# Expert MLPs with 608 slots each, six row buffers, and the router's logits and transpositions in one step

## The chip, the cores and the metric

The kernel runs on 1 core of one Trainium2 chip. The metric is device time in microseconds of one execution; before the change three runs were taken, and their median counts. Engines are named as in the profile: PE (TensorE matmuls), PEld (its weight loads), DVE (VectorE), ACT (ScalarE), POOL (GpSimd), SP (SyncE, which issues DMAs).

## The reference

Three layers follow each other, in fp32. Inputs: q, k, v of shape 4 x 8 x 576 x 64, a gated MLP with w_a, w_b (512 x 1536) and w_out (1536 x 512), and eight experts with w1 (512 x 1024) and w2 (1024 x 512) each.

```python
scores = scale * np.matmul(q, k.transpose(0, 1, 3, 2))
scores = np.where(masks[None, :, :, :], scores, -1000000000.0)   # heads 0-3 local, 4-7 strided
attn = np.exp(scores - np.max(scores, axis=-1, keepdims=True))
attn = attn / (np.sum(attn, axis=-1, keepdims=True) + 1e-09)
x = np.matmul(attn, v)                                            # as 2304 rows of 512
x = (x @ w_a) * (x @ w_b) @ w_out
noisy_logits = x @ w_gate + np.log1p(np.exp(x @ w_noise)) * noise
top2 = np.argpartition(-noisy_logits, 2, axis=1)[:, :2]
...
out[mask] += top2_w[mask, k, None] * (np.maximum(x[mask] @ w1[e], 0.0) @ w2[e])
```

Each of the 2304 tokens goes to its two best experts of eight, with softmax weights over the two; 576 tokens per expert on average.

## The kernel before, in words

**Products.** Every large product is made of three fp32r matmuls (`mm3`, L194 to L198): each operand is split into a high and a low part, and hi x hi (L196), lo x hi (L197) and hi x lo (L198) are summed. ACT makes the high part, DVE the low one.

**First stage.** Tokens are cut into five chunks: c = 0 to 3 hold the first 512 tokens of a batch, c = 4 holds the 64 last tokens of the four batches (256 columns). For each chunk, f runs over 12 blocks of the hidden width: `stage_a` (L691) makes pa and pb (12 matmuls each), whose product is split into gh and gl, and `stage_b` (L716) of the block before adds to the output po. `ORDER` (L557) gives the sequence. PE's order is written by hand in this stage; the order of ACT, DVE, POOL and SP is planned by a scheduler that works with its own model of durations. After pa, after pb and after po comes a call of `point()` (L797): it takes one step of attention (`attq`), one of `finq` (or a second of attention), and one of `bgq` (two in the last chunk). These queues hold generators; a step ends at a `yield`.

**Router.** When a chunk's rows are out, `finish(c, rows)` (L425) is put on `finq`. For each of the chunk's J tiles (four, two in the last chunk) it transposes the rows (four transposes into a PSUM tile of tag t, which has two buffers; copied to x2T by DVE or ACT, L432 to L437) in one step, and multiplies with the gate weights in the next (L441, copied to lg by DVE at L442). `route` (L446) then follows: a chain of small DVE and ACT operations that gives the two best experts of each token and their weights, up to ms (L478); after three yields the ranking product (L485) counts places within each expert; then slots are worked out (L489 to L507) and POOL scatters token numbers and weights into `table` in DRAM (L510). For the last chunk the experts 0 and 1 start at slot 384 or later (GAP), so that their tiles 0 to 2 can be fetched before it.

**Experts.** Each expert has CAP = 640 slots, five tiles of 128. `fetch` reads the table (L757, SP), gathers the rows of each tile from x2 (L763, POOL), transposes them (L772) and splits them into hi and lo (L773, L774). Tiles 0 to 2 are group 0 (384 columns), tiles 3 and 4 group 1 (256 columns). `passes` (L859) lists the work: the experts 0 and 1 go by groups in four passes (0: expert 0, tiles 0 to 2; 1: expert 1, the same; 2 and 3: the tiles 3 and 4 of both), the experts 2 to 6 in one pass each, and the last expert in two, the tiles 3 and 4 at the very end. In a pass, for each of 8 blocks f, `mm1` (L863) makes ph for each group (12 matmuls with the group's columns moving) and splits relu(ph) into hh (ACT, L872) and hl (DVE, L873); `mm2` (L878) follows LAG = 2 blocks later with three matmuls of 512 columns for each tile, the tile's 128 columns of hh and hl as weights. At the last block the row tile y is scaled (L894 DVE, L896 ACT; three buffers) and added to the output by a scatter on POOL (L897). In this stage the scheduler plans PE's order too.

**Weights.** `load_expert` (L731) reads w1 and w2 in pieces of 512 KB into two st buffers (L156, SP) and splits them (L159 ACT, L160 DVE); it runs on `bgq`, for expert 0 from c = 4, f = 4 on. Slots above CAP would be done by `overflow_tile` (L928), one tile at a time, if any expert has more tokens than CAP; a count decides at the end (L909, L920).

Of the kernel before, what the change touches and what calls it, by code (L numbers as in the profile page):

```python
# [20 lines left out]
NT = 2304  # L21
LAG = 2
PAD = 1024
CAP = 640
# [8 lines left out]
def attention_moe_kernel(ctx: ExitStack, tc: tile.TileContext, q, k, v, w_a, w_b, w_out,  # L33
# [15 lines left out]
    table = tc.dram_tile([E * NT, 2], I32, name="table")  # L49
# [16 lines left out]
    limit = cpool.tile([1, (NT - CAP) // 128], F32, name="limit")  # L66
# [13 lines left out]
    with tc.tile_pool(name="setup", bufs=1) as sp:  # L80
# [20 lines left out]
        nc.gpsimd.iota(base, pattern=[[NT, 8]], base=0, channel_multiplier=0,  # L101
                       allow_small_or_imprecise_dtypes=True)
        nc.gpsimd.iota(base0, pattern=[[NT, 8]], base=0, channel_multiplier=0,
                       allow_small_or_imprecise_dtypes=True)
        nc.gpsimd.iota(limit, pattern=[[128, (NT - CAP) // 128]], base=CAP, channel_multiplier=0,
# [16 lines left out]
    def late_setup():  # L122
        nrow = E * NT // 128
# [301 lines left out]
    def finish(c, rows):  # L425

        T0, J = tile_of(c)
        lg = rpool.tile([128, J, 16], F32, name="lg", tag="lg")
        for j in range(J):
            ps = pt([128, KD, 128])  # L430
            for kd in range(KD):
                nc.tensor.transpose(ps[:, kd, :], rows[j][:, 128 * kd:128 * kd + 128], ident)  # L432
            x2T = rpool.tile([128, KD, 128], F32, name="x2T", tag="x2T")
            if j % 2:
                nc.vector.tensor_copy(x2T, ps)
            else:
                nc.scalar.activation(x2T, ps, AF.Copy)  # L437
            yield
            ps = pt([128, 16])
            for kd in range(KD):  # L440
                nc.tensor.matmul(ps, x2T[:, kd, :], wg[:, kd, :], start=(kd == 0), stop=(kd == KD - 1))  # L441
            nc.vector.tensor_copy(lg[:, j, :], ps)  # L442
            yield
        yield from route(c, lg)

    def route(c, lg):  # L446
# [32 lines left out]
        yield  # L479
        yield  # L480
        yield
# [5 lines left out]
        if c == NCH - 1:  # L487
            for e in range(2):
                nc.vector.tensor_scalar(base[:, e:e + 1], base[:, e:e + 1], float(e * NT + GAP), None, op0=OP.max)  # L489
# [251 lines left out]

    def xset(e, g):
        n = 3 if g == 0 else 2
        p = xpool[e % 2, g]
        if (e, g) not in XS:
            t = f"x{g}{e % 2}"
            if p is rpool:
                both = p.tile([128, 2, KD, 128 * n], F32R, name=t, tag="row")
                XS[e, g] = (both[:, 0], both[:, 1])
                return XS[e, g]  # L750
            XS[e, g] = (p.tile([128, KD, 128 * n], F32R, name=t + "h", tag=t + "h"),
                        p.tile([128, KD, 128 * n], F32R, name=t + "l", tag=t + "l"))
        return XS[e, g]

    def load_table(e, t0, n):
        tb = rpool.tile([128, n, 2], I32, name="tb", tag="tb", bufs=6)
# [266 lines left out]
```

## Time and profile before

| what | value |
| --- | --- |
| runs | median 1139.32 us of 3 (1137.73 to 1145.32) |
| profiled execution, its own time | 1142.42 us |
| its span | 1140.6 us |
| granted TensorE clock, mean | 0.961 of full |
| instructions | 16116 |
| DMA | 105.02 MB, mean 92 GB/s |

The span runs from the first to the last instruction that the profile shows; the 1.8 us between it and the execution's own time lie around it. In the profile's rows times are microseconds from the span's start, and a mean duration is in ns. Matmuls are pipelined, so a matmul's drawn length overlaps the next one's; the pace is read from start to start. A row of the timeline may merge several like instructions (x8), and in square brackets it names how long the engine was idle before and what ended that.

### The profile page before, as it was taken

To read this page: it belongs to the slowest core of one execution; us is meant where nothing else is said; L and a number is where in the kernel's file an instruction comes from. 1 tells how busy PE (TensorE), PEld (TensorE's weight loads), DVE (VectorE), ACT (ScalarE), POOL (GpSimd) and SP (SyncE) were. 2 spreads that over 40 slices of the span, in tenths; PEclk is the share of its full clock that TensorE was granted. 3 is DMA by queue.
4 is the path that set the end of the run, shared out by engine and by line. 5 is a ranking of instruction groups with operands and counts; after the bars stand their busy time and mean duration, and the time that the engine had idled before them with its cause. 6 is when DMAs were issued, how large, how long until landed. Compare 5 with 4: busy or idle time off the path is not lost.

```text
span 1140.6 us, 16116 instructions
## 1 busy us (share of the span) xinstructions
PE 1097.2 (96%) x6411; PEld 929.8 (82%) x6411; DVE 511.5 (45%) x1075; ACT 432.3 (38%) x935; POOL 141.8 (12%) x136
## 2 busy tenths in 40 slices
PE   6989999999999999999997899989999999999996
PEld 4767777887778877888887799978999999999995
DVE  5849777735545444323135552245343334342211
ACT  4767877422333322212124532244242324241110
POOL 0000000002000020002002123221121313131111
PEclk7579999999999999999998999998999999999998
DMA  9535434200212021900003434266254635442123
GB/s 187 131 99 169 144 109 144 79 22 13 57 37 70 12 53 41 330 29 2 1 37 111 151 109 75 43 194 172 83 121 119 129 112 121 120 122 37 21 29 47
DMA packets 88549, 105.02 MB, mean 92 GB/s; under 512 B 43664, under 2 KB 48400, under 8 KB 88464
## 3 DMA queue, kind: packets, MB, share of 16 engines
q1 hardware_dynamic: 78352, 82.89, 24.5%
q0 software_dynamic: 10112, 21.02, 10.2%
q8 instruction: 52, 0.85, 0.3%
q14 instruction: 33, 0.27, 0.1%
HBM read 78.53 MB, written 25.35 MB: 91 GB/s over the span
## 4 chain that ended last, share of the span: by engine, by line
PE 81%; DVE 7%; DMA 6%; ACT 3%; issue 1%; another core or an unknown queue 1%; SPq 1%; POOL 0%; ACTq 0%; POOLq 0%; DVEq 0%
PE ph L196 6%; PE ph L198 6%; PE ph L197 6%; PE py L196 6%; PE py L197 6%; PE py L198 6%; PE pa L196 4%; PE pb L196 4%; PE po L196 4%; PE pb L197 4%; PE pb L198 4%; PE pa L197 4%; PE pa L198 4%; PE po L198 4%; PE po L197 4%; PE tt L290 2%
## 5 line engine op out<-in xcount | busy, mean ns | idle before, releaser
L873 DVE SCALAR_TENSOR_TENSOR hl<-ph,hh 128x256 fp32r<-128x256 f32 (+1 forms) x128 | 62.3, 489 | 213.9 <-ACT hh L872 212.6
L872 ACT ACTIVATE hh<-ph 128x256 fp32r<-128x256 f32 (+1 forms) x128 | 55.2, 433 | 225.0 <-PE ph L198 222.5
L708 DVE TENSOR_TENSOR a<-a,pb 128x512 f32<-128x512 f32 (+1 forms) x60 | 37.9, 632 | 130.5 <-PE pb L198 124.8
L897 POOL DMA_INDIRECT out_dram<-y,tb x40 | 64.0, 1600 | 185.7 <-ACT y L896 144.8
L510 POOL DMA_INDIRECT table<-pay,sli x36 | 35.1, 975 | 411.3 <-DVE sli L498 384.2
L703 ACT ACTIVATE a<-pa 128x512 f32<-128x512 f32 (+1 forms) x60 | 33.1, 551 | 120.4 <-PE pa L198 118.2
L763 POOL DMA_INDIRECT g<-x,tb x40 | 40.1, 1003 | 192.1 <-PE tt L772 170.0
L709 ACT ACTIVATE gh<-a 128x512 fp32r<-128x512 f32 (+1 forms) x60 | 35.1, 586 | 70.7 <-DVE a L708 57.2
L710 DVE TENSOR_TENSOR gl<-a,gh 128x512 fp32r<-128x512 f32 (+1 forms) x60 | 38.1, 635 | 20.0 <-ACT gh L709 18.8
L290 PEld LDWEIGHTS tt<-kT,qT 64*72 64x72 f32 (+1 forms) x336 | 29.5, 149 | 13.4 <-issue 10.3
L290 PE MATMUL tt<-kT,qT 64*72 64x72 f32 (+1 forms) x336 | 37.6, 253 | 1.1 <-ACT pT L336 1.1
L196 PE MATMUL py<-w6h,hh 128*128 128x512 f32 x80 | 32.3, 406 | 4.0 <-ACT hh L872 4.0
L336 ACT ACTIVATE pT<-tt 128x288 f32<-128x288 f32 (+1 forms) x64 | 24.9, 408 | 28.7 <-PE tt L335 28.7
L196 PE MATMUL pa<-xh,w0h 128*128 128x512 f32 (+1 forms) x80 | 32.7, 408 | 1.6 <-ACT xh L414 1.4
L335 PE MATMUL tt<-ident,s 72*72 72x72 f32 (+1 forms) x224 | 29.4, 263 | 4.2 <-DVE s L327 2.1
L335 PEld LDWEIGHTS tt<-ident,s 72*72 72x72 f32 (+1 forms) x224 | 22.3, 140 | 12.6 <-ACT qT L262 2.9
L196 PE MATMUL pb<-xh,w4h 128*128 128x512 f32 (+1 forms) x80 | 31.5, 394 | 0.6 <-issue 0.6
L197 PE MATMUL py<-w6l,hh 128*128 128x512 f32 x80 | 32.0, 400 | 0.0
L196 PE MATMUL pb<-xh,w1h 128*128 128x512 f32 (+1 forms) x80 | 31.9, 399 | 0.0
L196 PE MATMUL py<-w3h,hh 128*128 128x512 f32 x80 | 31.8, 398 | 0.0
L196 PE MATMUL py<-w2h,hh 128*128 128x512 f32 x80 | 31.8, 399 | 0.0
L196 PE MATMUL pa<-xh,w3h 128*128 128x512 f32 (+1 forms) x80 | 31.6, 395 | 0.0
(294 smaller groups left out, 3283.6 us busy)
## 6 DMA issues: line engine op xcount, KB each, us to landing
st<-in_moe_w_dram SPq DMA_DIRECT2D x64, 512.0 KB
out_dram<-zero SPq DMA_DIRECT2D x13, 512.0 KB
raw<-in_moe_w_a_dram SPq DMA_DIRECT2D x4, 1024.0 KB
raw<-in_moe_w_b_dram SPq DMA_DIRECT2D x4, 1024.0 KB
raw<-in_moe_w_out_dram SPq DMA_DIRECT2D x4, 1024.0 KB
x<-row SPq DMA_DIRECT2D x16, 256.0 KB
raw<-in_moe_w_a_dram SPq DMA_DIRECT2D x4, 512.0 KB
raw<-in_moe_w_b_dram SPq DMA_DIRECT2D x4, 512.0 KB
```

Of the source, the lines that this page charges most:

```text
L196: nc.tensor.matmul(ps, w[0], x[0], start=start, stop=False)
L197: nc.tensor.matmul(ps, w[0], x[1], start=False, stop=False)
L198: nc.tensor.matmul(ps, w[1], x[0], start=False, stop=stop)
L290: nc.tensor.matmul(ps[:, ii, :], self.qT[r0:r0 + 64, q0:q0 + n], self.kT[r0:r0 + 64, k0:k0 + m], start=not pemask, stop=not pemask or ii = ...
L335: nc.tensor.transpose(ps[:, ii, :], self.s[half][:, x, ii, :], ident[:n, :n])
L510: ins = nc.gpsimd.indirect_dma_start(out=table, out_offset=bass.IndirectOffsetOnAxis(ap=sli[:, 2 * j + kk:2 * j + kk + 1], axis=0), in_=pa ...
L708: nc.vector.tensor_mul(a, a, pb)
L710: behind[0] = nc.vector.tensor_sub(gl, a, gh.bitcast(F32))
L763: nc.gpsimd.indirect_dma_start(out=g, out_offset=None, in_=x2, in_offset=bass.IndirectOffsetOnAxis(ap=TB[e, t][:, 0:1], axis=0))
L872: nc.scalar.activation(hh, ph, AF.Relu)
L873: nc.vector.scalar_tensor_tensor(hl, ph, 0.0, hh.bitcast(F32), op0=OP.max, op1=OP.subtract)
L897: ins = nc.gpsimd.indirect_dma_start(out=out, out_offset=bass.IndirectOffsetOnAxis(ap=TB[e, t][:, 0:1], axis=0), in_=y, in_offset=None, co ...
```

## The change

1. CAP goes from 640 to 608, so tile 4 of each expert holds 96 rows and group 1 has 224 columns. `rows_of` and `WIDTH` give the sizes; table reads, gathers, transposes, splits, mm1, mm2, scaling and scatters use them. Each expert has 2400 places in the table instead of 2304, and the table's fill and the overflow's limits follow. `load_table` reads whole tiles with one DMA and tile 4 with its own.
2. The row tiles y have six buffers instead of three; the overflow's h takes a buffer of `ring` instead of its own.
3. In `finish`, the logits of one tile and the transposition of the next are one step, for every chunk: five steps for four tiles instead of eight, three for two instead of four. In `route`, the ranking product of c = 3 comes six yields after ms instead of three. Before steps of `first` (expert 0's fetch) are taken, `finq` is emptied.
4. At the very end, the two blocks of mm2 that are left are done tile by tile instead of block by block.

```diff
-CAP = 640
+CAP = 608
+SLOTS = 2400
...
-    table = tc.dram_tile([E * NT, 2], I32, name="table")
+    table = tc.dram_tile([E * SLOTS, 2], I32, name="table")
...
         lg = rpool.tile([128, J, 16], F32, name="lg", tag="lg")
-        for j in range(J):
-            ps = pt([128, KD, 128])
-            for kd in range(KD):
-                nc.tensor.transpose(ps[:, kd, :], rows[j][:, 128 * kd:128 * kd + 128], ident)
-            x2T = rpool.tile([128, KD, 128], F32, name="x2T", tag="x2T")
-            if j % 2:
-                nc.vector.tensor_copy(x2T, ps)
-            else:
-                nc.scalar.activation(x2T, ps, AF.Copy)
-            yield
-            ps = pt([128, 16])
-            for kd in range(KD):
-                nc.tensor.matmul(ps, x2T[:, kd, :], wg[:, kd, :], start=(kd == 0), stop=(kd == KD - 1))
-            nc.vector.tensor_copy(lg[:, j, :], ps)
+        x2T = None
+        for j in range(J + 1):
+            if j:
+                ps = pt([128, 16])
+                for kd in range(KD):
+                    nc.tensor.matmul(ps, x2T[:, kd, :], wg[:, kd, :], start=(kd == 0), stop=(kd == KD - 1))
+                nc.vector.tensor_copy(lg[:, j - 1, :], ps)
+            if j < J:
+                ps = pt([128, KD, 128])
+                for kd in range(KD):
+                    nc.tensor.transpose(ps[:, kd, :], rows[j][:, 128 * kd:128 * kd + 128], ident)
+                x2T = rpool.tile([128, KD, 128], F32, name="x2T", tag="x2T")
+                if j % 2:
+                    nc.vector.tensor_copy(x2T, ps)
+                else:
+                    nc.scalar.activation(x2T, ps, AF.Copy)
             yield
         yield from route(c, lg)
...
         ms = rpool.tile([128, J, 8], BF, name="ms", tag="ms")
         nc.vector.tensor_add(ms, oh[:, :, 0, :], oh[:, :, 1, :])
-        yield
-        yield
-        yield
+        for _ in range(6 if c == B - 1 else 3):
+            yield
         rk = pt([128, J + 1, 8])
...
+    def rows_of(t):
+
+        return min(128, CAP - 128 * t) if t >= 0 else 128
+
+    WIDTH = [384, CAP - 384]
+
     def xset(e, g):
-        n = 3 if g == 0 else 2
+        n = WIDTH[g]
...
-    def load_table(e, t0, n):
-        tb = rpool.tile([128, n, 2], I32, name="tb", tag="tb", bufs=6)
-        nc.sync.dma_start(tb, table[e * NT + 128 * t0:e * NT + 128 * (t0 + n), :].rearrange("(p t) c -> p t c", t=n))
-        for i in range(n):
-            TB[e, t0 + i] = tb[:, i, :]
+    def load_table(e, tiles):
+
+        whole = [t for t in tiles if rows_of(t) == 128]
+        for some in (whole, [t for t in tiles if rows_of(t) < 128]):
+            if some:
+                n, m, r0 = len(some), rows_of(some[0]), e * SLOTS + 128 * some[0]
+                tb = rpool.tile([128, n, 2], I32, name="tb", tag="tb" if some is whole else "tb4", bufs=5)
+                nc.sync.dma_start(tb[:m], table[r0:r0 + m * n, :].rearrange("(p t) c -> p t c", t=n))
+                for i, t in enumerate(some):
+                    TB[e, t] = tb[:m, i, :]
...
     def gather(e, t):
         g = xpool["g"].tile([128, DM], F32, name="g", tag="g", bufs=GB[0])
-        nc.gpsimd.indirect_dma_start(out=g, out_offset=None, in_=x2,
+        nc.gpsimd.indirect_dma_start(out=g[:rows_of(t)], out_offset=None, in_=x2,
                                      in_offset=bass.IndirectOffsetOnAxis(ap=TB[e, t][:, 0:1], axis=0))
...
     def spread(e, t, g):
         xh, xl = xset(e, int(t >= 3))
-        c0 = 128 * (t if t < 3 else t - 3)
-        ps = pt([128, KD, 128])
+        c0, n = 128 * (t if t < 3 else t - 3), rows_of(t)
+        ps = pt([128, KD, n])
         for kd in range(KD):
-            nc.tensor.transpose(ps[:, kd, :], g[:, 128 * kd:128 * kd + 128], ident)
-        nc.scalar.activation(xh[:, :, c0:c0 + 128], ps, AF.Copy)
-        nc.vector.tensor_sub(xl[:, :, c0:c0 + 128], ps, xh[:, :, c0:c0 + 128].bitcast(F32))
+            nc.tensor.transpose(ps[:, kd, :], g[:n, 128 * kd:128 * kd + 128], ident[:n, :n])
+        nc.scalar.activation(xh[:, :, c0:c0 + n], ps, AF.Copy)
+        nc.vector.tensor_sub(xl[:, :, c0:c0 + n], ps, xh[:, :, c0:c0 + n].bitcast(F32))
...
             if c == NCH - 1 and f in (8, 11):
+                while finq:
+                    advance(finq)
                 for _ in range(3 if f == 8 else 2):
                     next(first)
...
     def mm1(e, f, grp, both):
         xh, xl = XS[e, grp]
-        n = 128 * (3 if grp == 0 else 2)
+        n = WIDTH[grp]
...
-    def mm2(pi, f, h):
+    def mm2(pi, f, h, only=None):
...
-        for i, t in enumerate(tiles):
-            hp = h[int(t >= 3)]
+        some = [(i, t) for i, t in enumerate(tiles) if only in (None, i)]
+        for i, t in some:
             c0 = 128 * (t if t < 3 else t - 3)
-            mm3(outs[pi][i], tuple(x[:, c0:c0 + 128] for x in hp), w, f == 0, f == NF2 - 1)
+            n = rows_of(t)
+            mm3(outs[pi][i][:n], tuple(x[:, c0:c0 + n] for x in h[int(t >= 3)]), w, f == 0, f == NF2 - 1)
...
-                y = ep.tile([128, DM], F32, name="y", tag="y", bufs=3)
+            for i, t in some:
+                n = rows_of(t)
+                y = ep.tile([128, DM], F32, name="y", tag="y", bufs=6)
...
                 ins = nc.gpsimd.indirect_dma_start(
                     out=out, out_offset=bass.IndirectOffsetOnAxis(ap=TB[e, t][:, 0:1], axis=0),
-                    in_=y, in_offset=None, compute_op=OP.add)
...
+    NOV = (SLOTS - CAP) // 128
...
-        h = ep.tile([128, NF2, 128], F32, name="hf", tag="hf")
+        h = ring.tile([128, NF2, 128], F32, name="hf", tag="w5h")
...
-    for x in later:
-        mm2(*x)
+    for i in range(len(passes[-1][1])):
+        for x in later:
+            mm2(*x, only=i)
     overflow()
```

Left out: the same sizes in `xset`, the constants and the scaling of y.

## Rows read from the trace of the kernel before

**Rows 1.** The profile's page, part 1: busy time, share and instructions of each engine.
```profile
PE 1097.2 (96%) x6411; PEld 929.8 (82%) x6411; DVE 511.5 (45%) x1075; ACT 432.3 (38%) x935; POOL 141.8 (12%) x136
```

**Rows 2.** PE's own waits in the whole span: us in total, times, longest.
```profile
PE tt L485 <- DVE ms L478: 6.9, 1, 6.9
...
PE py L196 <- ACT hh L872: 4.0, 1, 4.0
PE ph L196 <- ACT x00h L773: 2.2, 1, 2.2
```

**Rows 3.** PE's timeline (start us, length us): first and twelfth matmul of two mm1 blocks.
```profile
904.47 0.28 PE L196 MATMUL ph<-x,w0h 128*128 128x256 f32 x1
...
905.78 0.28 PE L198 MATMUL ph<-x,w0l 128*128 128x256 f32 x1
...
1118.13 0.28 PE L196 MATMUL ph<-x11h,w5h 128*128 128x256 f32 x1
...
1119.40 0.28 PE L198 MATMUL ph<-x11h,w5l 128*128 128x256 f32 x1
```

**Rows 4.** Groups by form: busy us, mean ns of one, idle before.
```profile
L441 PEld LDWEIGHTS tt<-wg,x2T 128*128 128x128 f32 x144 | 18.0, 191 | 0.8
L290 PE MATMUL tt<-kT,qT 64*72 64x72 f32 x192 | 16.8, 232 | 0.0
L197 PEld LDWEIGHTS ph<-x00l,w1h 128*128 128x128 f32 x64 | 12.0, 188 | 0.6
L485 PEld LDWEIGHTS <-ones 128*128 128x128 bf16 x43 | 1.8, 98 | 0.0
```

**Rows 5.** Timeline of PE and its loads, last chunk, 602 to 622 us.
```profile
602.65 0.97 PEld L441 LDWEIGHTS tt<-wg,x2T 128*128 128x128 f32 x8
...
616.18 0.19 PE L485 MATMUL tt<-ms,tri 128*128 128x8 bf16 x1 [6.86 <-DVE ms L478]
...
616.93 0.41 PE L197 MATMUL pa<-xl,w3h 128*128 128x256 f32 x1
...
621.63 0.41 PE L198 MATMUL pb<-xh,w4l 128*128 128x256 f32 x1
```

**Rows 6.** Timeline of DVE and ACT in the same stretch.
```profile
604.92 0.17 DVE L442 COPY lg<-tt 128x16 f32<-128x16 f32 x1
...
608.01 0.69 DVE L160 TENSOR_TENSOR w1l<-st,w1h 128x512 fp32r<-128x512 f32 x1 [1.30 <-ACT w1h L159]
...
613.16 1.15 ACT L159 ACTIVATE w2h<-st 128x512 fp32r<-128x512 f32 x2 [1.51 <-DMA st<-in_moe_w_dram]
...
615.94 0.18 DVE L478 TENSOR_TENSOR ms<-oh 128x32 bf16<-128x32 f32 x1
615.96 1.15 ACT L159 ACTIVATE w2h<-st 128x512 fp32r<-128x512 f32 x2
```

**Rows 7.** Windows: length, busy of PE, PEld, DVE, ACT, POOL, granted clock, DMA share, GB/s.
```profile
618.00:620.00 2.00, 2.00 (x11) 2.00 (x11) 0.92 (x10) 0.38 (x1) 0.77 (x1) 0.50 0.78 200
656.00:658.00 2.00, 1.80 (x7) 1.54 (x8) 1.50 (x3) 0.14 (x1) 0.00 (x0) 0.53 0.69 171
```

**Rows 8.** Timeline of PE and ACT with attention, second and third chunk.
```profile
233.94 0.73 PE L290 MATMUL tt<-kT,qT 64*72 64x72 f32 x8
...
362.96 0.41 PE L258 MATMUL tt<-ident,ql 96*128 96x96 f32 x3
...
363.71 0.69 ACT L262 ACTIVATE qT<-tt 128x288 f32<-128x288 f32 x1
```

**Rows 9.** All waits, the row of ACT for a y buffer: us, times, longest.
```profile
ACT y L896 <- DMA out_dram<-y,tb: 9.0, 4, 3.8
```

**Rows 10.** POOL's timeline at the end: the last two scatters.
```profile
1130.12 1.55 POOL L897 DMA_INDIRECT out_dram<-y,tb  x1 [15.28 <-ACT y L896]
1131.98 1.55 POOL L897 DMA_INDIRECT out_dram<-y,tb  x1 [0.30 <-issue]
```

More of the change, by code (lines that the diff above doesn't have):

```diff
@@ L65, in attention_moe_kernel @@
     base0 = cpool.tile([1, 8], F32, name="base0")
-    limit = cpool.tile([1, (NT - CAP) // 128], F32, name="limit")
+    limit = cpool.tile([1, (SLOTS - CAP) // 128], F32, name="limit")
     ids = cpool.tile([128, NTL], I32, name="ids")
@@ L122, in late_setup @@
     def late_setup():
-        nrow = E * NT // 128
+        nrow = E * SLOTS // 128
         fill = rpool.tile([128, nrow, 2], I32, name="fill", tag="x2T")
@@ L488, in route @@
             for e in range(2):
-                nc.vector.tensor_scalar(base[:, e:e + 1], base[:, e:e + 1], float(e * NT + GAP), None, op0=OP.max)
+                nc.vector.tensor_scalar(base[:, e:e + 1], base[:, e:e + 1], float(e * SLOTS + GAP), None, op0=OP.max)
         sl = rpool.tile([128, J, 8], F32, name="sl", tag="sl")
@@ L747, in xset @@
             if p is rpool:
-                both = p.tile([128, 2, KD, 128 * n], F32R, name=t, tag="row")
+                both = p.tile([128, 2, KD, n], F32R, name=t, tag="row")
                 XS[e, g] = (both[:, 0], both[:, 1])
                 return XS[e, g]
-            XS[e, g] = (p.tile([128, KD, 128 * n], F32R, name=t + "h", tag=t + "h"),
-                        p.tile([128, KD, 128 * n], F32R, name=t + "l", tag=t + "l"))
+            XS[e, g] = (p.tile([128, KD, n], F32R, name=t + "h", tag=t + "h"),
+                        p.tile([128, KD, n], F32R, name=t + "l", tag=t + "l"))
         return XS[e, g]
-    def load_table(e, t0, n):
-        tb = rpool.tile([128, n, 2], I32, name="tb", tag="tb", bufs=6)
-        nc.sync.dma_start(tb, table[e * NT + 128 * t0:e * NT + 128 * (t0 + n), :].rearrange("(p t) c -> p t c", t=n))
-        for i in range(n):
-            TB[e, t0 + i] = tb[:, i, :]
+    def load_table(e, tiles):
[7 more added lines that the diff above has]
+                    TB[e, t] = tb[:m, i, :]
     def gather(e, t):
         g = xpool["g"].tile([128, DM], F32, name="g", tag="g", bufs=GB[0])
-        nc.gpsimd.indirect_dma_start(out=g, out_offset=None, in_=x2,
+        nc.gpsimd.indirect_dma_start(out=g[:rows_of(t)], out_offset=None, in_=x2,
                                      in_offset=bass.IndirectOffsetOnAxis(ap=TB[e, t][:, 0:1], axis=0))
@@ L928, in overflow_tile @@
     def overflow_tile(e, i):
-        tb = rpool.tile([128, 1, 2], I32, name="tb", tag="tb", bufs=6)
-        nc.sync.dma_start(tb[:, 0, :], table[ds(e * NT + CAP + i * 128, 128), :])
+        tb = rpool.tile([128, 1, 2], I32, name="tb", tag="tb4", bufs=5)
+        nc.sync.dma_start(tb[:, 0, :], table[ds(e * SLOTS + CAP + i * 128, 128), :])
         TB[e, -1] = tb[:, 0, :]
@@ L952, in overflow_tile @@
             nc.tensor.matmul(py, h[:, f, :], w[2 + f // 4][:, f % 4, :], start=(f == 0), stop=(f == NF2 - 1))
-        y = ep.tile([128, DM], F32, name="y", tag="y", bufs=3)
+        y = ep.tile([128, DM], F32, name="y", tag="y", bufs=6)
         nc.vector.tensor_scalar(y, py, tb[:, 0, 1:2].bitcast(F32), None, op0=OP.mult)
```

22 lines of the change are left out of this document (10 added, 12 removed).

## The prediction

> **What bounds the kernel now.** First the page's busy line: PE works 1097.2 of the 1140.6 us span, every other engine under half of it [rows 1]. A busy PE says only that there is work in it, so the list of PE's own waits came next: three are long, 6.9 us for ms before the ranking product (L485), 4.0 us for hh (py, L196) and 2.2 us for x00h (ph, L196) [rows 2]. Elsewhere the matrix products stand end to end, so a microsecond is won either by making the stream of matmuls shorter or by taking one of these waits away. The timelines then give the pace of the stream (start to start, the drawn lengths overlap) and show the 6.9 us wait from close by.
>
> **Narrower mm1.** Width 256 becomes 224 in group 1: 4 kd x 3 products = 12 matmuls for each of 8 f and 8 experts, 768 in all. Their pace now: 905.78 - 904.47 over 11 steps is 119 ns, 1119.40 - 1118.13 over 11 steps 115.5 ns [rows 3]; I use 117.5. If time went with columns alone, 32 of 256 would save 117.5/8 = 14.7 ns each, 11.3 us in all; that is the upper end. But each matmul has its own weight load of 128 columns, and those have a pace too: L441's four products are issued as eight pairs of load and matmul of only 16 columns, whose loads take 0.97 us together; with the last one's 191 ns off, (0.97 - 0.19)/7 = 111 ns each [rows 4, 5]. They are plain fp32, but a load lasts 191 ns there and 188 ns in mm1, against 98 ns in bf16 [rows 4], so I take them for equal. Then the pace can't fall below 111 ns: 6.5 ns x 768 = **5.0 us**. If 117.5 is already the handover of loads, it is 0; if the pace rises instead, this is the rival on the other side, below.
>
> The Trainium skill ("TensorE: Matmul & The Clock Gate", LDWEIGHTS) puts a load at its columns over 1.2 GHz, 106.7 ns for 128; L441's 111 ns agrees. By that figure the saving would be (117.5 - 106.7) x 768 = 8.3 us, an estimate. The same page (Weight-path perf modes) says that a fast weight load is on for 128 weights that are not FP32. If that held for these fp32r operands there would be no floor near 111 ns; mm1's 188 ns beside bf16's 98 [rows 4] speaks against it.
>
> **What else narrows.** Transposing tile 4 moves 96 columns instead of 128: 8 experts x 4 transposes, at most a quarter of about 110 ns each, under 0.9 us; I take 0.3. mm2 still moves 512 columns per product, its narrower weight load lies under them: 0. Evictions, gathers and scatters get shorter on engines that are under half busy: 0 on the path, and a few hundred ns at worst if that cover is gone. The count of tokens matters first: counting the reference's two choices for its inputs gives 600, 568, 578, 583, 594, 563, 565, 557 per expert, so none passes 608 and no overflow tile runs. The split table load adds one SP DMA where tile 4 is fetched together with others; it waits for the same as the first, and the weight loads queued behind it on SP move by one issue: 0, with splits that wait for these loads paying it at worst. For a gain there no reason shows.
>
> **finish() of the fourth chunk.** A turn is one call of point(). Now the eight logit and transposition turns end at turn 8, route's vector chain is turn 9, the ranking product turn 12. After it they end at turn 5, the chain is turn 6, and with six yields the product is still turn 12, at the same place in PE's order. So PE's work ahead of it is unchanged and only the chain starts earlier: by three blocks of 12 matmuls at 115.5 ns (or 6 of twice the width), 4.2 us. Now the last logits start at 602.65 on PE, are copied at 604.92 because weight splits (L160) stand ahead on DVE, and ms comes at 615.94 + 0.18: 11.2 us, with splits of w1 and w2 in between that wait for ACT and by it for loads, 1.30 us in one place [rows 5, 6]. PE goes on at 616.18 after 6.86 us idle, so it was ready at 609.3 [rows 5]. With an unchanged chain from about 599.8 (PE's logits 4.2 us earlier and no split ahead, since w0 is split only after turn 7) ms would be there at 611.0: 1.7 us late; a chain that meets fewer splits is not late at all. I take 1.0 us left.
>
> The wait also costs clock. After it the granted clock is 0.50 in 618 to 620 [rows 7], and the 256-column pace is (621.63 - 616.93)/22 = 214 ns [rows 5]: 24 matmuls at 98 ns over 115.5 are 2.4 us, with the first of po 2.7. So wait and clock cost 9.6 us, all of it to be had at most. What is late next: DVE and ACT run in order, and the splits of w2 wait for loads that land at 613.16 and let ACT go on at 615.96 [rows 6]. If the next eviction of pa stays behind them, PE, no longer held at the ranking, stops there: pa of the f after would wait until 615.96 + 1.15 + 0.4 for its own copy, 617.5, with PE ready three blocks after the ranking, at 613.9: 3.6 us, and with a slow stretch after it about 6.6. So the part is worth 3 to 9.6 us; I take **8.0** (1.0 left at the ranking, 0.6 at pa), since the chain no longer lies among the splits that wait for loads. Scatters, the table load behind them on SP and the weight loads behind that all follow the ranking at the same distance, so they move with it: 0.
>
> **finish() of the others.** Logits and the next transposition now use both PSUM buffers of tag t in one turn, while attention (first two chunks) uses one in the same turn; the transposition waits until attention's tile is copied. That copy ended at 363.71 + 0.69 = 364.40, its products started at 362.96 and took 0.41, and logits of about 0.97 would stand between [rows 5, 8]: 1.03 us of copy against 0.97, 0.1 us late, more where DVE is busy. Six such turns: **+1.0 us** (0 to 3).
>
> **Six y buffers and the last pass.** ACT's waits for a y buffer sum to 9.0 us in 4 [rows 9], but none appears among PE's waits [rows 2]: 0, and 1 or 2 us if the shorter stream had brought them out. In the last 12 products, tile 3's three for f = 7 come 3 x 0.23 us earlier, twice the 256-column pace each, so its copy and its scatter (1130.12) too; the second scatter follows the first on POOL at 1131.98 [rows 10] and moves as much, 0.7, and has 96 rows: **0.9 us** (0.7 to 2.5).
>
> **Eaten again.** The 4.0 us wait for hh [rows 2] falls in the fourth pass, where ACT stands behind splits that wait for loads. What the third and fourth passes gain, 2 x 96 x 6.5 ns = 1.2 us, mostly lengthens it: **+1.0 us** (0 to 1.2).
>
> Sum: 5.0 + 0.3 + 8.0 - 1.0 + 0.9 - 1.0 = 12.2 us. Against the profiled execution's own 1142.42 us (span 1140.6 and 1.8 around it) this is 1130.2. That execution is 3.1 us above the median of the runs, 1139.32, so the forecast is 1139.3 - 12.2 = **1127.1 us**.
>
> **Rivals.** (a) The gain is given back: the loads hold the pace at 117.5 (0) and the evictions of pa stop behind w2's splits (3): 0.3 + 3 - 1 + 0.9 - 1 = 2 us, 1137. For it: the loads pace ACT there [rows 6]. Against: the chain leaves the stretch in which they land. (b) All comes: 11.3 by columns, 9.6, 2.5 and 0.9, less 1: 23 us, 1116. Against it stands L441's pace. (c) Slower: below 256 columns fp32r falls to the pace of plain fp32. The trace has no fp32r matmul under 256 columns. Plain fp32 takes (0.73 - 0.23)/7 = 71 ns for 72 columns, with the last one's 232 ns off, and its four products are eight instructions [rows 4, 8]; at that rate 224 columns cost 221 ns, twice 442. Even once, 221 - 117.5 = 103 ns x 768 = 79 us, less the other 7.2: +72 us, 1211. It decides from about 142 ns per matmul on ((11.4 + 7.2)/768 = 24 ns more). Against it: no row shows a width at which the pace changes its kind, and an fp32r product is one instruction at every width here. (d) Also slower: the order that is planned for ACT and DVE changes with the width, puts splits ahead of hh where loads are late, and waits like the 4.0 us one, with the slow clock after it (0.53 of full after the 2.2 us one [rows 7]), come 4 more times at 6 us: 24 - 12.2 = +12, 1151. (e) An overflow tile runs: excluded by the counts.
>
> **Chances.** Forecast with its spread (1121 to 1134) 0.54, (a) 0.19, (b) 0.15, (c) 0.04, (d) 0.08. About 1% (11.4 us, so 1127.9) is what a measurement of this kernel can tell from no change. The forecast lies just past that line, so 0.32 of its 0.54 count as faster and 0.22 as the same. Faster: 0.32 + 0.15 = 0.47. Same: 0.22 + 0.19 = 0.41. Slower: 0.04 + 0.08 = 0.12. Range: from (b) to a little past no change, 1115 to 1141, which takes in the bounds of the terms and leaves out (c), (d) and the outermost of the rest.
>
> **What would show it.** Right: 224-column pace 108 to 113 ns, the wait of L485 for ms under 2 us and no 0.50 clock after 610, ph groups of 224 columns summing 5 us less, the first scatter of the last pass 0.7 us nearer the last matmul. Wrong: a pace over 117 ns; a new wait of PE for ACT a or hh between 605 and 625; a longer wait at the start of expert 2.

## The result, and the profile after

The changed kernel takes 1126.94 us (median of 4 runs, 1123.0 to 1130.01), the kernel before 1138.53 us on the same chip: ratio 0.9884, 95% interval 0.9848 to 0.9921. The forecast was 1127.1 us. The total came out; several of its terms did not, and two of them cancelled.

First the page's busy line of the changed kernel, to be set beside [rows 1]:

```profile
PE 1086.5 (97%) x6411; PEld 914.2 (82%) x6411; DVE 508.5 (45%) x1075; ACT 430.1 (38%) x935; POOL 141.7 (13%) x136
```

PE still bounds it, with the same 6411 instructions. The profiled execution took 1123.0 us, the fastest of the four, while the one shown of before took 1142.42, above its median. The two profiles therefore differ by 19.4 us where the medians differ by 11.6, and no sum is made from the two alone. The list of PE's own waits in the changed kernel answers to [rows 2]:

```profile
...
PE py L197 <- ACT hh L887: 2.3, 1, 2.3
PE pa L197 <- ACT a L705: 2.3, 2, 2.0
PE ph L197 <- ACT x00h L786: 2.2, 1, 2.2
...
PE pb L197 <- DVE a L710: 1.8, 1, 1.8
```

The 6.9 us for ms are gone. Two waits in the last chunk, for the evictions of pa and pb, have come instead (before, PE waited 0.5 us for ACT's copies of pa there and not for pb's). Left out at the head of this list are waits of attention in the stage ahead of c = 1, which both kernels have; before, the largest of them was

```profile
PE sc L258 <- ACT s L323: 6.6, 3, 3.5
```

PE's timeline of the changed kernel in the last mm1 block, with columns as in [rows 3], shows the pace at 224 columns:

```profile
1105.87 0.27 PE L197 MATMUL ph<-x11h,w5h 128*128 128x224 f32 x1
...
1107.09 0.28 PE L199 MATMUL ph<-x11h,w5l 128*128 128x224 f32 x1
```

(1107.09 - 1105.87)/11 = 110.9 ns. The mean over the 702 pairs of neighbouring products of this width in the whole trace is 110.9 too, against 117.5 for the 256 columns before.

The last chunk of the changed kernel by DVE's, ACT's, PE's and POOL's timelines (start us, length us), to be set beside [rows 5, 6]:

```profile
594.28 0.17 DVE L436 COPY lg<-tt 128x16 f32<-128x16 f32 x1 [0.31 <-PE tt L435]
...
602.40 0.19 DVE L481 TENSOR_TENSOR ms<-oh 128x32 bf16<-128x32 f32 x1
...
604.08 0.18 PE L487 MATMUL tt<-ms,tri 128*128 128x8 bf16 x1
...
608.58 0.97 POOL L512 DMA_INDIRECT table<-pay,sli  x1 [87.25 <-DVE sli L500]
...
617.64 0.97 POOL L512 DMA_INDIRECT table<-pay,sli  x1 [0.30 <-issue]
...
618.51 1.15 ACT L160 ACTIVATE w3h<-st 128x512 fp32r<-128x512 f32 x2 [3.79 <-DMA st<-in_moe_w_dram]
619.56 0.36 ACT L705 ACTIVATE a<-pa 128x256 f32<-128x256 f32 x1
...
619.98 0.38 PE L197 MATMUL pa<-xh,w 128*128 128x256 f32 x1 [2.03 <-ACT a L705]
...
628.02 0.39 PE L197 MATMUL pb<-xh,w 128*128 128x256 f32 x1 [1.83 <-DVE a L710]
```

ms stands 1.5 us before the ranking product, which waits for nothing. But ACT then waits 3.79 us for a weight load, the copy of pa stands behind that split (619.56), and PE stops. Around POOL's scatters of the table (608.58 to 618.6) and behind the second stop, windows of the changed kernel show this (columns as in [rows 7]):

```profile
604.00:608.00 4.00, 4.00 (x43) 3.85 (x42) 3.36 (x12) 2.16 (x5) 0.00 (x0) 1.00 0.62 199
608.00:612.00 4.00, 4.00 (x30) 3.78 (x30) 2.25 (x6) 1.48 (x4) 2.81 (x3) 1.00 0.52 151
612.00:616.00 4.00, 3.70 (x27) 3.15 (x26) 2.05 (x4) 1.81 (x4) 3.08 (x4) 1.00 0.80 57
616.00:620.00 4.00, 1.97 (x12) 1.37 (x10) 0.83 (x2) 1.42 (x3) 2.00 (x3) 1.00 0.64 203
620.00:624.00 4.00, 3.98 (x28) 3.52 (x29) 2.42 (x5) 1.83 (x4) 0.00 (x0) 1.00 0.67 66
...
628.00:632.00 4.00, 3.70 (x15) 2.95 (x16) 2.36 (x5) 1.84 (x4) 2.39 (x2) 0.61 0.60 188
```

In one window beside the scatters the DMA engines are busier than ahead of them (0.80 against 0.62) and move 57 GB/s instead of 199. The windows on either side, which have scatters too, move 151 and 203, and the next one, in which POOL does nothing, 66; so it isn't shown that the scatters are what slows the loads. Behind the stop for pb the granted clock is 0.61 of full. The end, POOL's last two scatters, answers to [rows 10]:

```profile
1112.32 1.56 POOL L914 DMA_INDIRECT out_dram<-y,tb  x1 [15.03 <-ACT y L913]
1114.18 1.43 POOL L914 DMA_INDIRECT out_dram<-y,tb  x1 [0.30 <-issue]
```

To compare stages over more than one pair of profiles, all kernels of this study stand in one table. The stages are cut in PE's timeline at the first pa of c = 1, the first pa of c = 4, the first ph and the end of the last py. All are in us of one profile each; the ratio is that of the runs. Every ratio is against the kernel before on the same chip, measured beside that run, so the time of before differs a little from run to run.

| kernel | ratio to before (95%) | c = 1 to 3 | c = 4 | experts | end |
| --- | --- | --- | --- | --- | --- |
| before | 1 | 370.4 | 74.6 | 473.1 | 11.3 |
| router's edit alone | 0.9966 (0.9954 to 0.9978) | 368.4 | 73.0 | 472.0 | 11.0 |
| six yields alone | 0.9972 (0.9954 to 0.9990) | 371.4 | 69.9 | 471.6 | 10.7 |
| five y buffers alone | 1.0003 (0.9992 to 1.0014) | 370.8 | 74.8 | 470.6 | 11.1 |
| 608 slots alone | 1.0051 (1.0031 to 1.0071) | 370.9 | 74.6 | 476.4 | 9.7 |
| after, three y buffers | 0.9998 (0.9982 to 1.0013) | 369.5 | 73.4 | 477.9 | 9.8 |
| after, four y buffers | 0.9920 (0.9894 to 0.9947) | 368.7 | 70.7 | 467.2 | 9.7 |
| **after** | 0.9884 (0.9848 to 0.9921) | 368.5 | 70.2 | 465.1 | 9.7 |
| after, last blocks as before | 0.9907 (0.9887 to 0.9927) | 369.6 | 70.5 | 467.4 | 9.4 |
| after, three yields | 0.9920 (0.9899 to 0.9942) | 369.4 | 72.1 | 468.3 | 10.2 |
| after, splits held back | 0.9917 (0.9901 to 0.9933) | 369.5 | 69.1 | 469.6 | 9.8 |
| after, one loader step | 0.9887 (0.9864 to 0.9909) | 368.7 | 71.3 | 467.1 | 9.8 |
| after, 576 slots | 0.9904 (0.9874 to 0.9934) | 369.3 | 71.0 | 468.0 | 8.4 |

The stage ahead of c = 1 lies between 207.1 and 211.2 us in these profiles, in no order that follows the edits; it carries 3.5 of the 19.4 us and is left out.

How far one profile can be trusted is seen from kernels that turn out to run the same instructions. On every engine the traces of "last blocks as before" and "one loader step" hold the same instructions in the same order as that of the changed kernel; their c = 4 takes 70.5 and 71.3 us beside its 70.2, and their experts 467.4 and 467.1 beside its 465.1. And seven kernels (the router's edit alone, three and four y buffers, after, the two just named and 576 slots) go through c = 4 with PE, ACT and DVE in the same order, and take between 70.2 and 73.4 us for it. So differences of 2 to 3 us in one stage are not resolved by a pair of profiles.

### The profile page after: what moved, and what is told of

It reads as the page before. It is cut to its first block, busy times and chain, and to the rows that moved or that the text cites. A ratio compares the mean times of both kernels' runs of the same rounds, so it can differ in the third digit from the quotient of the medians.

```text
span 1121.2 us, 16112 instructions
## 1 busy us (share of the span) xinstructions
PE 1086.5 (97%) x6411; PEld 914.2 (82%) x6411; DVE 508.5 (45%) x1075; ACT 430.1 (38%) x935; POOL 141.7 (13%) x136
## 5 line engine op out<-in xcount | busy, mean ns | idle before, releaser
L888 DVE SCALAR_TENSOR_TENSOR hl<-ph,hh 128x224 fp32r<-128x224 f32 (+1 forms) x128 | 60.1, 472 | 207.3 <-ACT hh L887 207.1
L887 ACT ACTIVATE hh<-ph 128x224 fp32r<-128x224 f32 (+1 forms) x128 | 53.4, 419 | 216.8 <-PE ph L199 216.8
L197 PE MATMUL py<-w7h,hh 128*128 128x512 f32 (+1 forms) x80 | 31.9, 399 | 2.3 <-ACT hh L887 2.3
L197 PE MATMUL pa<-xh,w 128*128 128x512 f32 (+1 forms) x80 | 30.6, 383 | 2.0 <-ACT a L705 2.0
L197 PE MATMUL pb<-xh,w 128*128 128x512 f32 (+1 forms) x80 | 30.7, 383 | 1.8 <-DVE a L710 1.8
L197 PE MATMUL py<-w2h,hh 128*128 128x512 f32 (+1 forms) x80 | 32.2, 402 | 0.0
L197 PE MATMUL py<-w3h,hh 128*128 128x512 f32 (+1 forms) x80 | 32.0, 400 | 0.0
L197 PE MATMUL py<-w6h,hh 128*128 128x512 f32 (+1 forms) x80 | 32.0, 400 | 0.0
L198 PE MATMUL py<-w3l,hh 128*128 128x512 f32 (+1 forms) x80 | 31.6, 395 | 0.0
L198 PE MATMUL py<-w2l,hh 128*128 128x512 f32 (+1 forms) x80 | 31.6, 395 | 0.0
```

What stands on the lines that cost most here:

```text
L197: nc.tensor.matmul(ps, w[0], x[0], start=start, stop=False)
L198: nc.tensor.matmul(ps, w[0], x[1], start=False, stop=False)
L887: nc.scalar.activation(hh, ph, AF.Relu)
L888: nc.vector.scalar_tensor_tensor(hl, ph, 0.0, hh.bitcast(F32), op0=OP.max, op1=OP.subtract)
```

## The experiments

**The router's edit alone.** The kernel before with the merged steps of `finish`, the six yields and the emptying of `finq`:

```diff
+        for j in range(J + 1):
+            if j:
...
+            if j < J:
...
             yield
...
-        yield
-        yield
-        yield
+        for _ in range(6 if c == B - 1 else 3):
+            yield
...
+                while finq:
+                    advance(finq)
```

> The kernel before with the router's part of the change alone: logits and the next transposition in one step, the fourth chunk's ranking six yields after ms, finq emptied first; 640 slots, three y buffers, old end. Theory A (the parts add, and about half of the router's gain comes back as waits for weight loads): the wait of 6.9 us at the ranking product and the slow clock after it are gone (9.6 us), new waits of PE for a in the last chunk cost 4 to 6, so 4 to 5 us faster, near 1134. Rival B (the router's part is the whole gain): 10 to 12 us faster, near 1127. Rival C (it comes back whole): within 2 us of before.

Measured: 1135.02 against 1138.98 us, ratio 0.9966. That is 3.9 us, where the prediction's two terms for this edit make 8.0 - 1.0 = 7.0. In the list of PE's waits of this kernel from 577 to 651 us, the last chunk, the wait for ms is gone, but others are new:

```profile
PE po L196 <- ACT gh L710: 3.5, 2, 2.2
...
PE pa L196 <- ACT w3h L159: 1.7, 1, 1.7
PE pb L196 <- DVE a L709: 1.5, 1, 1.5
```

The wait was not removed as a whole; part of it moved to the evictions, which stand behind weight splits.

**608 slots alone.** The kernel before with the 608 slots, three y buffers, the old `finish` and the old end:

```diff
-CAP = 640
+CAP = 608
+SLOTS = 2400
```

> The change's 608 slots alone: old steps in the router, three yields, three y buffers, old end. Theory A: the pace of group 1's matmuls is 111 ns for 224 columns instead of 117.5, 5 us, the 512-column products cost some 2 us more, the ranking wait of about 7 us stays: 3 to 5 us faster, near 1135. Rival B: nothing, within 2 us of before. Rival C (time goes with columns): pace 103 ns, 11 us faster.

Measured: 1145.04 against 1138.98 us, ratio 1.0051, slower by 5.8 us. The pace at 224 columns is 110.9 ns here too, so the 5 us of narrower products are in this kernel and some 10 are lost beside them. The experts' stage shows where: 476.4 us against 471.8 in the mean of the four kernels at 640 slots. Half of the loss stands in PE's waits as waits for copies into y, 4.5 us here and 0.7 more for DVE's copies:

```profile
PE tt L784 <- ACT y L910: 4.5, 3, 1.9
```

**The changed kernel with three y buffers.**

```diff
-                y = ep.tile([128, DM], F32, name="y", tag="y", bufs=6)
+                y = ep.tile([128, DM], F32, name="y", tag="y", bufs=3)
```

> The changed kernel with three y buffers instead of six. Theory A (with 608 slots the plan for the engines puts copies of y where a scatter still holds the buffer; the six buffers pay for that): waits of y for out_dram are back, 20 to 30 us on ACT and DVE, some of them reach PE by the PSUM bank that tile 4 shares with the transpositions: 6 to 11 us slower than the changed kernel, 1133 to 1138. Rival F (the buffers are idle and something else made the run with 608 slots alone slow): within 2 us of the changed kernel.

Measured: 1139.2 against 1139.03 us, ratio 0.9998: without the buffers the whole change is worth nothing. Its waits, where [rows 9] had 9.0 us and PE had none for y:

```profile
ACT y L913 <- DMA out_dram<-y,tb: 18.3, 4, 6.0
...
DVE y L911 <- DMA out_dram<-y,tb: 11.3, 5, 4.4
...
PE tt L785 <- ACT y L913: 4.7, 3, 1.6
...
PE py L197 <- DVE y L911: 0.6, 1, 0.6
```

One such place in its timeline, where expert 4's pass ends:

```profile
958.10 1.82 POOL L914 DMA_INDIRECT out_dram<-y,tb  x1 [18.36 <-DVE y L911]
...
958.91 0.40 PE L199 MATMUL py<-w3h,hl 128*96 128x512 f32 x1
...
960.22 1.56 POOL L914 DMA_INDIRECT out_dram<-y,tb  x1 [0.30 <-issue]
...
965.38 0.75 DVE L911 TENSOR_SCALAR y<-py,tb 128x512 f32<-128x512 f32 x1 [1.63 <-DMA out_dram<-y,tb]
...
968.05 0.68 ACT L913 ACTIVATE y<-py,tb 96x512 f32<-96x512 f32 x1 [4.50 <-DMA out_dram<-y,tb]
...
968.79 0.66 PE L785 MATMUL tt<-ident,g 128*128 128x128 f32 x4 [1.63 <-ACT y L913]
```

The same place in the kernel before:

```profile
961.22 0.39 PE L198 MATMUL py<-w3h,hl 128*128 128x512 f32 x1
...
969.30 0.69 ACT L896 ACTIVATE y<-py,tb 128x512 f32<-128x512 f32 x1 [0.22 <-DVE w3l L160]
...
970.47 0.60 PE L772 MATMUL tt<-ident,g 128*128 128x128 f32 x4
```

Tile 4's py lies in a PSUM buffer of tag t, the tag of the transpositions. In the order planned for 256 columns, 51 products lie between the last one of expert 4's pass (961.22) and the next transposition (970.47), and PE is never idle between them; in the order planned for 224 columns there are 39 (958.91 to 968.79). With three y buffers tile 4's copy has to wait until the second scatter, begun at 960.22, has landed (968.05, 7.8 us later). Before, PE had work for that time; now it stands for 0.65 us ahead of a product of expert 5, which needs tile 3's PSUM buffer, and for 1.63 ahead of the transposition; and ACT, which waits 4.50 us for the scatter, has the next hh behind that copy. A product of 224 columns is only 6.6 ns shorter, which is far too little for this, so the order that came with the width is the likely cause; no run has the old order at 224 columns, and why the planner chose the new one was not looked into.

Six buffers change PE's order in the experts' stage once more. At this place 25 products then lie between, fewer still, and PE doesn't stop, since tile 4's copy (945.12) waits for no scatter; so here it is the buffers that take the wait out. In the whole stage PE is idle for 10.6 us with three buffers and for 2.5 with six, and runs at half clock for 6.8 us with three and not at all with six: together some 11.5 of the 12.8 us by which the two profiles differ there.

**Five y buffers alone.** The control at 640 slots. Six don't fit there, so it has five; the overflow's h lies in `ring` as in the change:

```diff
-                y = ep.tile([128, DM], F32, name="y", tag="y", bufs=3)
+                y = ep.tile([128, DM], F32, name="y", tag="y", bufs=5)
...
-        h = ep.tile([128, NF2, 128], F32, name="hf", tag="hf")
+        h = ring.tile([128, NF2, 128], F32, name="hf", tag="w5h")
```

> The kernel before with five y buffers (six don't fit beside 640 slots) and the overflow's h in a buffer of ring, nothing else. As forecast: waits for y fall from 18.8 us to near 0 but none of them reached PE: 0, within 1.5 us of before. Rival G (the buffers are worth as much without the 608 slots): 6 to 10 us faster.

Measured: 1139.44 against 1139.03 us, ratio 1.0003. At 640 slots the buffers are worth nothing, as forecast; ACT's and DVE's waits for them disappear and nobody had waited behind these. (PE's order in the experts' stage is not that of before here either.)

**Four y buffers.** The changed kernel with one more than before:

```diff
-                y = ep.tile([128, DM], F32, name="y", tag="y", bufs=6)
+                y = ep.tile([128, DM], F32, name="y", tag="y", bufs=4)
```

> The changed kernel with four y buffers instead of six. With three it took 1139.2 us, 12 over the six: the copies of the fourth and fifth tile of a pass waited for a scatter to land and PE's transposition waited for the fifth copy. If only the number of copies in a pass counts, five tiles for three buffers, the fourth buffer takes the wait off one of two copies and about half comes back, 1131 to 1134. If the fifth copy alone holds PE, its buffer is then the first tile's, whose scatter has one more of 1.9 us to land: nearly all comes back, 1127 to 1130.

Measured: 1131.16 against 1139.64 us, ratio 0.9920 (four runs, the profiled one 1127.84). The time lies at the edge between the two expectations, the profile on the side of the second: the experts take 467.2 us against 477.9 with three and 465.1 with six, PE's list has no wait for y, and in ACT's there is left

```profile
ACT y L913 <- DMA out_dram<-y,tb: 5.9, 3, 4.0
```

So the fourth buffer gives back most; the times don't resolve what the fifth and sixth add.

**The ranking at turn 9.** The changed kernel with the three yields of before in all chunks:

```diff
-        for _ in range(6 if c == B - 1 else 3):
-            yield
+        yield
+        yield
+        yield
```

> The changed kernel with three yields before the fourth chunk's ranking instead of six, so it comes at turn 9 and not 12. Theory A (the six yields are what gives the chain its time): the chain still ends near 602.6, PE comes to the ranking about 4 us earlier, so a wait of 3 to 5 us for ms is back, with some clock; the table and the loads behind it come 3 us earlier: 2 to 6 us slower than the changed kernel. Rival E (the merged steps alone do it, the yields nothing): within 1 us of the changed kernel.

Measured: 1129.94 against 1138.98 us, ratio 0.9920. PE waits 2.6 us for ms again, and c = 4 takes 72.1 us instead of 70.2. The six yields are worth some 2 us beside the merged steps by c = 4 and some 4 by the two ratios; neither the ratios' intervals nor the spread of c = 4 among equal programs lets either number stand for sure.

**The ranking at turn 15.** The kernel before with the six yields and no merged steps:

```diff
-        yield
-        yield
-        yield
+        for _ in range(6 if c == B - 1 else 3):
+            yield
...
+                while finq:
+                    advance(finq)
```

> The kernel before with the six yields of the fourth chunk alone; logits and transpositions stay in steps of their own, so the ranking product comes at turn 15 instead of 12. Both parts of the router's edit together gave 1135.02 us, 3.9 under before. If room between ms and the ranking is all that counts, the chain starts where it did, the product waits for nothing and PE's wait for ms goes: about 1135 again, ratio 0.996 to 0.998, and the stretch from the second chunk to the last stays at 370 us, since nothing is merged there. If the chain has to leave the stretch in which w1 and w2 are split, the place behind them only moves the stop: table, scatters and expert 0's weights all come three blocks later, and the time is that of before or more, 1138 to 1143.

Measured: 1137.04 against 1139.64 us, ratio 0.9972. Room alone gives most of what the router's edit gives, with neither expectation wholly right: the wait for ms is shorter, not gone.

```profile
PE tt L484 <- DVE ms L478: 3.0, 1, 3.0
```

ms was there at 616.1 before and PE went on at 616.18; here PE goes on at 617.29. The chain ends no earlier than it did; PE reaches the ranking later, with three blocks done in between. c = 4 is 4.7 us shorter in these two profiles, where the runs give 2.6 us in all. The stretch from c = 1 to c = 3 is where it was (371.4): in the four kernels without merged steps it is 370.4 to 371.4 us, in the nine with them 368.4 to 369.6.

**The splits held back.** In the changed kernel the loader's steps of the last chunk are issued behind the block's gl, one of two per turn:

```diff
-                advance(bgq)
                 if c == NCH - 1:
+                    with tc.issue_after(behind[0].ins):
+                        advance(bgq)
+                else:
                     advance(bgq)
```

> The changed kernel with one step of expert 0's weight loads per turn in the last chunk instead of two, issued after the latest gl. If the waits of PE for a in the last chunk (2.0 and 1.8 us, and the half clock after the second) are splits that stand ahead of evictions and wait for loads, they go, and it is 3 to 6 us faster than the changed kernel, near 1122; later weights could make expert 0 wait at its start instead, then within 2 us. If they come from the loads' pace itself, nothing is won.

Measured: 1129.54 against 1139.03 us, ratio 0.9917. The last chunk is the shortest of all (69.1 us, not by more than its spread), but the experts take 469.6. Of PE's waits, the first of these two lies in the last chunk, where PE still stops for evictions of pa (5.3 us; 2.3 in the changed kernel, and 1.8 for pb), and the second in the experts' stage:

```profile
PE pa L197 <- ACT a L705: 5.3, 2, 3.9
PE py L197 <- ACT hh L889: 4.6, 2, 3.8
```

What isn't split ahead of the experts is split among their first passes: at 664.91 ACT starts w6h after 3.70 us of waiting for its load, with hh behind it.

**One loader step per turn.**

```diff
-                if c == NCH - 1:
-                    advance(bgq)
```

> The changed kernel with one step of the weight loader per turn in the last chunk instead of two, so the splits of expert 0's weights are spread over twice the turns. If the two short stops of PE for pa and pb in the last chunk (2.0 and 1.8 us, with the slow clock after them) come from splits that wait for their loads ahead of the evictions, they go and the kernel is 2 to 5 us faster than the changed one: 1122 to 1125. If the loads of expert 0 are then late for its first passes, it is slower: weights that PE waits for at the start of the experts, 1130 and more.

Measured: 1128.12 against 1139.64 us, ratio 0.9887, the same as the changed kernel. The wait of PE for pa is still 2.0 us and ACT's w3h split still waits 3.73 us for its load. But this is no answer to the question: the trace holds the same instructions in the same order on every engine as the changed kernel's, so the edit spread no split. It is a second measurement of the changed kernel, and whether spread splits would help stays untested.

**The last blocks as before.**

```diff
-    for i in range(len(passes[-1][1])):
-        for x in later:
-            mm2(*x, only=i)
+    for x in later:
+        mm2(*x)
```

> The changed kernel with the last two blocks of mm2 in the old order, block by block. As forecast: the first of the two last scatters starts 0.7 us later against the last matmul, and the end comes 0.7 to 0.9 us later. Rival: the second scatter waits for POOL either way and has 96 rows; nothing, within 0.4 us by the trace.

Measured: 1127.61 against 1139.03 us, ratio 0.9907, no difference that these runs resolve. The first of the last scatters starts 0.77 us behind the end of the last product here (1115.30 - 1114.53) and in the changed kernel (1112.32 - 1111.55), and 0.77 before. PE does both tiles' last products interleaved in all three: the planner sets PE's order in this stage, and the two orders of the calls give the same instructions in the same order on every engine, so this too is a second measurement of the changed kernel.

**192 columns.** The changed kernel with 576 slots; what it leaves out are the tokens beyond the 576th of an expert, and the overflow.

```diff
-CAP = 608
+CAP = 576
...
-    overflow()
```

> The changed kernel with 576 slots, so group 1 has 192 columns; tokens beyond 576 of an expert are left out, and so is the overflow at the end. Theory A (the weight load of 128 columns sets the pace): the pace stays at 109 to 111 ns, and the time is that of the changed kernel within 3 us. Rival C (columns set it, 0.21 ns per column from 256 to 224): 32 columns less give another 6.6 ns, pace 104, 5 us faster than the changed kernel. Rival D (columns at full slope): pace 97, 10 us faster.

Measured: 1127.71 against 1138.98 us, ratio 0.9904, not faster than 608 slots. PE's timeline, first and twelfth product of a block:

```profile
1109.88 0.25 PE L197 MATMUL ph<-x11h,w5h 128*128 128x192 f32 x1
...
1111.08 0.27 PE L199 MATMUL ph<-x11h,w5l 128*128 128x192 f32 x1
```

(1111.08 - 1109.88)/11 = 109 ns, and 109.8 in the mean over 702 pairs. The step from 256 to 224 columns brought 6.6 ns per product, the next 32 columns 1.1: the pace has a floor close under 111 ns.

## Why the prediction held, and which of its steps did not

The total, from means over kernels that share a part: c = 1 to 3 takes 370.9 us in the four kernels without merged steps and 369.1 in the nine with them, -1.8. c = 4 takes 74.7 us in the three with the old `finish` and 70.7 in the mean of the changed kernel and its versions with four buffers, one loader step or the old end, -4.0; with the three other kernels that go through it in the same order the mean is 71.4, -3.2. The experts take 471.8 us in the four kernels at 640 slots and 466.5 in the changed kernel and the two last named, -5.3; the end -1.4. That makes -12.5 us (-11.7 with the wider mean), where the medians give -11.6 and the ratio -13.2. Forecast was -12.2. That the sum comes so close is in part luck: two terms of some 10 us and more, put at nothing in the sum, cancelled, and the router's two terms were off in opposite directions.

| step of the prediction | forecast us | measured us | by |
| --- | --- | --- | --- |
| narrower mm1 | -5.0 | -5.1 | 768 x (117.5 - 110.9) ns |
| finish() of the fourth chunk | -8.0 | -3 to -4 | c = 4 |
| finish() of the others | +1.0 | -1.8 | c = 1 to 3 |
| six y buffers | 0 | about -13 at 608 slots, 0 at 640 | three against six; five alone |
| order of the planned stream at 224 columns | 0 (rival (d)) | some +10 with three buffers, 1.8 of it the slower products of 512 columns | 608 slots alone, +4.6 (experts) to +5.8 (runs) and the 5.1 of mm1 |
| last pass | -0.9 | -1.4 | the end |
| eaten again at pass 4 | +1.0 | not seen | wait for hh 2.3 us |

**Narrower mm1** held, size and reason: the pace fell to the load's floor and 192 columns hardly went below. The sum by columns (11.3 us) is refuted. Rival (c) did not come. Nor did the estimate of 8.3 us from the Trainium skill ("TensorE: Matmul & The Clock Gate", LDWEIGHTS) come out: its 106.7 ns was reached at neither width.

**finish() of the fourth chunk** failed in its last step. The wait and its clock were nearly all won at first: from f = 1 to f = 6 PE takes 26.9 us (581.9 to 608.8) against 36.1 before (587.2 to 623.3), 9.2 of the 9.6 that the prediction had put as the upper end. From there to the first ph it takes 37.6 us against 32.9. I had priced the stop behind the splits at 0.6; it is 4.7 in this profile, and 4.7 to 8.0 in those of the seven kernels with the same order. The prediction's own sign of being wrong, a new wait of PE for ACT's copy of pa between 605 and 625, is there at 619.98 (2.03 us). The step that failed is "so they move with it: 0" for scatters, table load and weight loads. The weight loads don't follow the ranking; they begin where expert 0's loader is queued, at f = 4, whose first pa starts at 599.8 (before, at 605.0). The SP queue's timeline of the kernel before:

```profile
603.50 14.88 SPq L156 DMA_DIRECT2D st<-in_moe_w_dram  x6
630.80 0.82 SPq L757 DMA_DIRECT2D tb<-table  x2
```

and of the changed kernel:

```profile
599.42 21.44 SPq L157 DMA_DIRECT2D st<-in_moe_w_dram  x7
623.75 0.82 SPq L770 DMA_DIRECT2D tb<-table  x2
```

The first scatter came 10.6 us earlier (608.58, before 619.23), the loads only 4.1 (599.42, before 603.50); 5.4 us of both is that c = 4 itself begins earlier in this profile (576.2, before 581.6). Before, six loads had been issued when the scatters began, the next came only behind the table read (632.66), and in ACT's timeline no split stands between 617.1 and 630.68, when the split of w3 starts without waiting for a load; so pa's copies in that stretch met none. Now the scatters fall among the loads, and the same split (618.51) waits for its load ahead of pa's copy. Whether the scatters slow the loads stays open: one window beside them moves 57 GB/s, its neighbours 151 and 203, and one without them 66, and it was not tried alone. Holding the splits back did not win it; spreading them was not reached by the run meant for it.

**finish() of the others** has the wrong sign. I had counted what the merged turn adds (a transposition that waits for a PSUM buffer) and not what it takes away, three turns of eight. Where in these chunks the 1.8 us come from was not taken apart, and the cause stays open.

**Six y buffers** is the largest miss, and by luck it did not show, since its opposite was missed with it. "None appears among PE's waits: 0" is true of the order of before, as five buffers alone show. But the change alters that order, and in the new one three buffers cost what everything else brings. Rival (d), a planned order that waits, comes nearest, priced at +12 us and a chance of 0.08; but it named splits ahead of hh, and what waits here are copies of y, for scatters that still hold their buffers. The slots alone fall into it (1.0051), and the buffers are what takes them out. The parts don't add: -3.9 (router), +5.8 (slots) and +0.3 (buffers, ratio 1.0003) sum to +2.2 us, and all together give -13.2.

**Last pass.** Of its two reasons the first was wrong: the order of the calls changes nothing. The second holds, and is worth more than was put on it. The end got shorter as the last scatter has 96 rows: from its start to the end of the span it is 7.0 us (1121.2 - 1114.18) where 128 rows took 8.6 (1140.6 - 1131.98).

**Eaten again** fell away: the wait for hh is 2.3 us, and 2.2 to 2.6 in the three other kernels at 640 slots, so what the 4.0 us of [rows 2] have above that belongs to that one execution.

**The list of waits.** The prediction reads three long waits from it and says that elsewhere the products stand end to end. The list's second row, 6.6 us of attention waiting for ACT ahead of c = 1, was passed over. It carries none of the terms, as the change doesn't touch that stage.

## What to carry to other kernels

A wait of an engine off the path costs nothing only in the order in which it was seen; where a planner makes the order anew, ask for each scarce buffer what stands behind it in the worst order, and give it room before the change is judged. Test a change's parts alone and together: here each half is worth little or less than nothing without the other. When a moving dimension is narrowed, look for the pace of the weight load first, since here it was the floor of the gain. Where a planner makes the order, compare the two traces' instructions before reading an experiment: two of the edits here changed nothing.

## What the runs showed of the hardware that I had not expected

The products of 512 columns got slower: 229.9 ns from start to start before, 231.8 after, and 231.4 to 232.5 in all profiles read at 608 or 576 slots, 229.7 to 230.0 in all at 640. It is not tile 4's narrower weights: pairs of tile 4 alone take 232.0 ns, those of whole tiles 231.7. Over 960 such products it is 1.8 us lost. Nor is it confined to the experts: in the first stage, whose widths are the same in all kernels, po's products take 229.4 to 229.7 ns at 640 slots and 230.9 to 231.2 in all at 608 or 576, pa's of 256 columns in c = 4 117.0 to 117.5 and 118.9 to 119.3, while pa's of 512 columns go the other way, from some 231.7 to some 231.1. So it isn't the width of the products themselves; the cause stays open.

The last scatter's time goes with its rows: from the last product to the end of the span 10.7 to 11.3 us for 128, 9.4 to 10.2 for 96 and 8.4 for 64. A scatter of 128 rows held its y buffer for 7.3 and 7.8 us from its start on POOL (958.10 to 965.38 and 960.22 to 968.05, with three buffers).
